# Inverse deviations by a GpSimd power, resident FFN weights from the third set of tokens on, and new constants in the planner's time model

## The chip, the cores and the metric

The kernel runs on one core of a Trainium2 chip. The metric is the device time of one execution in microseconds (us), as the median of several runs. The engines are named as in the profile: PE (TensorE, matmuls), PEld (its weight loads), DVE (VectorE), ACT (ScalarE), POOL (GpSimd) and SP (SyncE, which here issues nearly all DMAs). Each engine executes its own instructions in order and waits on semaphores for the others.

## The reference

One transformer block with modulation from a condition vector, for 2048 tokens of width 512, with 32 heads of 16 and an FFN of width 1792, in bfloat16:

```python
x = A_x
mod = (_silu(c) @ w_mod).reshape(c.shape[0], 6, 1, -1)
sa, ca, ga, sb, cb, gb = (mod[:, i] for i in range(6))
h = _layernorm(x, axis=-1) * (1 + ca) + sa
x = x + ga * _A_ref(h, A_wqkv, A_wo)        # softmax attention over all 2048 keys, then wo
h = _layernorm(x, axis=-1) * (1 + cb) + sb
x = x + gb * _B_ref(h, B_w_gate, B_w_up, B_w_down)
# _B_ref: _gelu(x @ w_gate) * (x @ w_up) @ w_down, with the tanh form of gelu
# _layernorm: (x - m) / sqrt(v + 1e-5), over the 512 of a token
```

## The kernel before

The program is written by a recorder. `rec` (L190) takes every instruction with what it reads and writes, works out the semaphores that it needs, and gives it a start and an end in a time model (`model`, L278). The order of the instructions of each engine is the order in which they are recorded, and a greedy planner (`stream`, L1224) chooses it: at each step it probes what each candidate would have to wait for in the model, and records one. A DMA's landing in the model is the end of the modelled DMA plus `LAND`, and the modelled DMA moves 350 bytes a nanosecond. Nothing of the plan is decided at run time.

The tokens are cut into sets of 512, 512, 512, 256, 128 and 128 queries (`SETS`). A unit is one set (the last two together for most heads) with four of the eight groups of heads; its scores come in rounds of four items, an item being 512 scores on all 128 partitions, in PSUM. There are 2048 items. Normally PE makes three of them, ACT takes their exps in one instruction (128 x 1536, PSUM to the SBUF tile `E`), and PE multiplies them with the values (`ps_pv`). Some rounds, called quads, go to DVE instead: it makes an approximate exp of each of the four items through a uint16 conversion (into the tiles `kq`, in `mreg` and `dreg`), and three shifted copies of 128 x 2048 uint16 (`shift_task`), which DVE or POOL makes and which PE multiplies with the values too. `QA` and `QB` say which tiles of keys may be treated so: a round must lie within them. `AHEAD` says how many items ahead of the current one a quad's round must lie at least. A quad is opened only where DVE is free in the model and one of three `kq` buffers is; after the scores of the third set (`ends[2]`), also only if the side work's credit is below `CREDIT` or its next matmul is not ready within `IDLE` (2000 ns, the flag `idle`).

Everything else is side work in the gaps of the attention: first the projections, then, for each set that is done, the output projection (`side_wo`), the second layernorm (`ln2_steps`) and the FFN (`side_ffn`), in the order and with the due times of `plan` (L1137). Small steps for DVE, ACT and SP are tasks, which `step` records when the model says that they would not wait. Softmax denominators go through DRAM: SP stores the sums (`scr_den<-osb`), loads them back spread over partitions (`den<-scr_den`), DVE takes reciprocals (`rden`), SP stores them (`scr_rec<-rden`) and loads them broadcast (`rb<-scr_rec`); then DVE makes the normalised output (`onorm`).

The inverse deviation of a layernorm (`ln_rstd`, L641, and `ln_rstd_step`, L627) is eight DVE instructions: a first guess through the bits of the number, then two Newton steps of three. It is called for four tiles of 128 tokens, or for as many as a set has, ten times in all.

An FFN of a set below `FLOW` (4) streams its weights: seven blocks of 256 KB of each of gate, up and down; gate and up through two buffers each (`wst`, in `mreg`), down into `wdst`. The last two sets use weights that stay (`wg`, `wu`, `wd`), 21 blocks, which `more_weights` loads once the third and the fourth FFN are done; the FFN of the fifth set waits for all of them (the key `weights`):

```python
    def more_weights(self):
        for parts, k in ((self.early, 2), (self.late, 3)):
            if parts and ("ffn", k) in self.have:
                parts.pop(0)()
                if not self.late:
                    self.done("weights")
                return True
        return False
```

They lie in memory that the attention no longer needs: the gate blocks in `qT` (queries of the first three sets), the down blocks in `xs` (tokens that have been put out), the up blocks in the streaming buffers.

After the last P·V comes `tail` (L1594): the fifth set's FFN, whose output projection, layernorm and transposes (`t2T`) must be recorded before it (the key `part`), and the sixth set's output projection, layernorm and FFN.

Of the kernel before, what the change touches and what calls it, by code (L numbers as in the profile page):

```python
# [13 lines left out]
P = 128  # L14
# [28 lines left out]
AHEAD = 24  # L43
PREFER = 300
LAND = 1500
# [10 lines left out]
QA = 6  # L56
QB = 13
FLOW = 4
# [37 lines left out]
class _Recorder:  # L96
# [181 lines left out]
    def model(self, op, t, cost):  # L278
        eng = op.eng
        if op.stream not in COMPUTE:  # L280
            self.free[eng] = t + 460
            self.dma_free = max(t + 1400, self.dma_free) + cost / 350
            op.t1 = self.dma_free + LAND
# [176 lines left out]
class _Kernel(_Recorder):  # L460
# [12 lines left out]
    def alloc(self):  # L473
# [25 lines left out]
        self.wdst = [dreg[:, a * D:(a + 2) * D] for a in (8, 10, 12)] + [mreg[:, a * D:(a + 2) * D] for a in (2, 0, 6, 4)]  # L499
        self.wdst = [a.rearrange("p (f n) -> p f n", f=2) for a in self.wdst]  # L500
        self.wg = [self.qT[:, :, 256 * i:256 * i + 256] for i in range(6)]
        self.wg.append(hreg[:, NFC * 256:NFC * 256 + 1024].rearrange("p (a n) -> p a n", a=NDC))
        self.wu = [self.wst[i // 2][i % 2] for i in range(4)]
        self.wu += [dreg[:, 1024 * i:1024 * i + 1024].rearrange("p (a n) -> p a n", a=NDC) for i in range(4, 7)]
        self.wd = [self.xs[:, 2 * i:2 * i + 2, :] for i in range(6)]
        self.wd.append(hreg[:, NFC * 256 + 1024:NFC * 256 + 2048].rearrange("p (f n) -> p f n", f=2))
# [15 lines left out]
        self.nwx = sb("nwx", [P, NT], FP32)  # L522
# [20 lines left out]
    def prologue(self):  # L543
# [19 lines left out]
        self.memset(dve, self.ones, 1.0)  # L563
        self.memset(dve, self.pv[:, :], 0.0)
# [60 lines left out]
    RSTD = 8  # L625

    def ln_rstd_step(self, a, b, i):  # L627

        x, y, t = self.nwx[:, a:b], self.rstd[:, a:b], self.nwt[:, a:b]
        if i == 0:  # L630
            self.ts("dve", x, self.mv[:, a:b, 1], EPS, -0.5, ALU.add, ALU.mult)
        elif i == 1:
            self.ts("dve", y.bitcast(I32), x.bitcast(I32), -0.5, 1597463007.0 - 2.0 ** 30 - 2.0 ** 22, ALU.mult, ALU.add)
        elif i % 3 == 2:
            self.tt("dve", t, y, y, ALU.mult)
        elif i % 3 == 0:
            self.tt("dve", t, t, x, ALU.mult)
        else:
            self.stt(y, t, 1.5, y, ALU.add, ALU.mult)

    def ln_rstd(self, a, b):  # L641
        for i in range(self.RSTD):
            self.ln_rstd_step(a, b, i)
# [145 lines left out]
    def side_first(self):  # L789
# [4 lines left out]
        def norms(t0):  # L794
            g = t0 // 4
            self.task([lambda i=i: self.ln_rstd_step(t0, t0 + 4, i) for i in range(self.RSTD)]
                      + [lambda t=t: self.ln_norm(t0 + t, self.tb1[:, g % 2, t, :]) for t in range(4)], ("ln", g),
                      self.after([("st", t) for t in range(max(8, t0), t0 + 4)]))
# [65 lines left out]
    def weight_parts(self):  # L864

        def part(dst, src, sem):
            return lambda: self.dma("sp", dst, src, sem)
# [3 lines left out]
        a = [part(self.wg[i], gv[:, :, 256 * i:256 * i + 256], "wg%d" % i) for i in range(7)]  # L871
        a += [part(self.wd[i], dv[:, 2 * i:2 * i + 2, :], "wd%d" % i) for i in range(7)]
        b = [part(self.wu[i], uv[:, :, 256 * i:256 * i + 256], "wu%d" % i) for i in range(7)]
        return a, b
# [4 lines left out]
    def ln2_steps(self, k, src=None):  # L879

        a, b = SETS[k][0] // P, sum(SETS[k]) // P
        return ([lambda i=i: self.ln_rstd_step(a, b, i) for i in range(self.RSTD)]
# [48 lines left out]
    def side_wo(self, gi):  # L931
# [14 lines left out]
        if not self.dry:  # L946
            self.done(("wo", gi))
            steps = self.ln2_steps(gi)
            self.task(steps[:self.RSTD], ("rs", gi), self.after([("st2", t) for t in tiles]))
            self.task(steps[self.RSTD:], ("ln2", gi), self.after([("rs", gi)] + [("ffn", gi - 1)] * (gi > 0)))  # L950

    def side_ffn(self, gi, part=None):
# [7 lines left out]
        flow = gi < FLOW  # L960
        kpb = 512 // W
# [5 lines left out]
        def load(x, ci):  # L967
            if flow and ci < len(chunks) and not self.dry:
# [9 lines left out]
        if flow:  # L978
            for i in range(2):
                load(0, i)  # L980
                load(1, i)
        yield from self.until(("ln2", gi))
        if not flow:
            yield from self.until("weights")
# [4 lines left out]
        def up(x, ci, sub):  # L989
            for s, fc in enumerate(sub):  # L990
                for dci in range(NDC):
                    if flow:
# [6 lines left out]
        def G(ci):  # L999
# [3 lines left out]
            if flow:  # L1003
                yield from self.until(("ld", gi, 0, ci))
# [13 lines left out]
        def U(ci):  # L1018
# [4 lines left out]
            if flow:  # L1023
                yield from self.until(("ld", gi, 1, ci))
            for b0 in range(0, m, kpb):
# [22 lines left out]
        if part is not None:  # L1048
            self.done(("part", gi))
            return  # L1050
        for i in range(n):
            for fc in range(NFC):
                yield 512, lambda i=i, fc=fc: self.mm(
                    mi, prod[:, fc, P * i:P * i + P], self.wdst[fc // 2][:, fc % 2, :], start=(fc == 0), stop=(fc == NFC - 1))
# [62 lines left out]
    def background(self, t):  # L1117
        if POOLED and self.free["pool"] < t and self.busy():
            self.pooled(t)
        while self.step("sp", max(self.free["sp"], t) + 40):  # L1120
            pass
        while self.free["dve"] <= t + 150 and self.step("dve", max(self.free["dve"], t) + 40):
            pass

    def force(self):
        assert any(self.step(e, None) for e in ("dve", "sp", "act")) or self.more_weights()

    def more_weights(self):
        for parts, k in ((self.early, 2), (self.late, 3)):
            if parts and ("ffn", k) in self.have:  # L1130
                parts.pop(0)()
                if not self.late:
                    self.done("weights")
                return True
# [611 lines left out]
```

## Time and profile before

| | us |
|---|---|
| median of 8 runs | 820.86 (818.78 to 823.49) |
| the profiled execution | 819.25 |
| its span in the profile | 817.5 |
| ACT's last exp of scores ends | 790.9 |
| outputs of set 3 (256 tokens) go out | 768.3 and 774.9 |
| outputs of set 2 go out | 696.7 to 720.7 |

The page in forty slices of 20.4 us; each digit is a busy share in tenths, and the last row is what the DMA moved:

```profile
DVE  7978999988898989998898999998887998776574
ACT  4999999999999999999999999999999999998972
POOL 1000623353362323614443424233020000000000
...
GB/s 313 50 8 12 16 10 16 10 16 10 15 61 34 55 59 36 59 42 23 28 61 54 35 60 34 61 41 22 30 22 117 61 62 64 23 210 208 89 95 15
```

A group's row later in the text reads: line, engine, operation, tile written and tiles read, shape, count, then busy time in us and the mean of one in ns, then the engine's idle time before these instructions and what ended it. Since a helper records each operation, all instructions of one kind have one line, and the tiles tell them apart. In a view of one tile, three numbers after a count are the shortest, the median and the longest in ns. A row of a stretch has its start and end, its length, and for each engine the busy time and the count, then PE's granted clock, the share of time in which the DMA engines were busy, and GB/s.

### The profile page before, as it was taken

Reading aid. Unit: us, or ns where it says so; the run is one execution under the profiler, and the core shown is the slowest. Engines: PE = TensorE matmul, PEld = TensorE weight load, DVE = VectorE, ACT = ScalarE, POOL = GpSimd, SP = SyncE. Lnnn points to the kernel's source line nnn. Section 1 sums busy time; section 2 is a strip of 40 time slices with the busy share of each in tenths; the row PEclk is TensorE's granted clock in tenths of the full one; section 3 lists DMA queues with packets and bytes.
Section 4 is the critical chain, followed back from the end, with each engine's and each line's share of the span. In section 5 each row is a group of like instructions: output and inputs, shape, how many; then the busy total and the mean of one; then the engine's idle time right before and its main releaser. Section 6 shows DMA issues by size and latency. Waiting matters only on the chain.

```text
span 817.5 us, 27542 instructions
## 1 busy us (share of the span) xinstructions
PE 752.6 (92%) x12273; PEld 268.6 (33%) x12278; DVE 695.6 (85%) x1320; ACT 779.7 (95%) x734; POOL 204.9 (25%) x118
## 2 busy tenths in 40 slices
PE   8899999999898899999998899999998899998988
PEld 3333333322222222222222222222343343445456
DVE  7978999988898989998898999998887998776574
ACT  4999999999999999999999999999999999998972
POOL 1000623353362323614443424233020000000000
PEclk9999999999999999999999999999999999999999
DMA  9100000000021121210122121210104222077330
GB/s 313 50 8 12 16 10 16 10 16 10 15 61 34 55 59 36 59 42 23 28 61 54 35 60 34 61 41 22 30 22 117 61 62 64 23 210 208 89 95 15
DMA packets 74569, 45.74 MB, mean 56 GB/s; under 512 B 18553, under 2 KB 71026, under 8 KB 74450
## 3 DMA queue, kind: packets, MB, share of 16 engines
q1 hardware_dynamic: 72066, 42.41, 18.8%
q8 instruction: 96, 1.57, 0.8%
q10 hardware_dynamic: 2384, 1.57, 0.7%
q14 instruction: 23, 0.19, 0.1%
HBM read 39.31 MB, written 2.61 MB: 51 GB/s over the span
## 4 chain that ended last, share of the span: by engine, by line
ACT 73%; PE 14%; DMA 5%; DVE 5%; SPq 3%; issue 1%; DVEq 0%
ACT E L367 70%; PE ps_mi L354 6%; PE ps_sc L354 6%; SPq L418 3%; ACT wreg L367 2%; PE ps_pv L354 2%; DMA mreg<-in_B_w_up_dram 1%; DMA scr_rec<-rden 1%; DMA mreg<-in_w_mod_dram 1%; DMA mreg<-in_B_w_gate_dram 1%; DVE mreg L379 1%; DMA den<-scr_den 1%; DVE wreg L371 1%; DMA scr_den<-osb 0%; DVE wreg L379 0%
## 5 line engine op out<-in xcount | busy, mean ns | idle before, releaser
L367 ACT ACTIVATE E<-ps_sc 128x1024 bf16<-128x1024 f32 (+2 forms) x687 | 751.2, 1271 | 22.4 <-PE ps_sc L354 21.6
L379 POOL TENSOR_SCALAR mreg<-dreg 128x2048 uint16<-128x2048 uint16 x78 | 146.8, 1897 | 257.5 <-PE ps_pv L354 53.9
L379 DVE TENSOR_SCALAR dreg<-ps_sc 128x512 uint16<-128x512 f32 x247 | 168.0, 687 | 28.0 <-PE ps_sc L354 25.1
L354 PE MATMUL ps_sc<-qT,kme 32*128 32x512 bf16 (+2 forms) x1321 | 166.3, 331 | 15.6 <-ACT E L367 13.7
L354 PE MATMUL ps_sc<-qT,kmo 32*128 32x512 bf16 (+2 forms) x1315 | 166.9, 332 | 12.1 <-ACT E L367 11.1
L354 PE MATMUL ps_pv<-E,vaug 128*17 128x512 bf16 (+2 forms) x2132 | 152.1, 327 | 1.3 <-DVE vaug L388 0.8
L354 PE MATMUL ps_mi<-wreg,mreg 128*32 128x512 bf16 (+1 forms) x1792 | 118.0, 359 | 11.6 <-DVE wreg L384 4.1
L354 PE MATMUL ps_pv<-mreg,vaug 128*17 128x512 bf16 (+2 forms) x1644 | 119.8, 342 | 3.1 <-DVE mreg L379 1.9
L379 DVE TENSOR_SCALAR mreg<-ps_sc 128x512 uint16<-128x512 f32 x129 | 87.9, 687 | 17.4 <-PE ps_sc L354 16.1
L354 PEld LDWEIGHTS ps_sc<-qT,kme 32*128 32x128 bf16 x1321 | 44.1, 91 | 138.7 <-ACT E L367 115.8
L354 PEld LDWEIGHTS ps_sc<-qT,kmo 32*128 32x128 bf16 x1315 | 44.1, 91 | 133.9 <-ACT E L367 111.0
L379 DVE TENSOR_SCALAR mreg<-dreg 128x2048 uint16<-128x2048 uint16 x129 | 84.6, 684 | 1.4 <-PE ps_pv L354 1.1
L379 POOL TENSOR_SCALAR mreg<-mreg 128x2048 uint16<-128x2048 uint16 x29 | 54.6, 1898 | 87.7 <-DVE mreg L379 66.2
L354 PEld LDWEIGHTS ps_pv<-E,vaug 128*17 128x17 bf16 x2132 | 45.0, 89 | 62.4 <-issue 50.6
L354 PEld LDWEIGHTS ps_mi<-wreg,mreg 128*32 128x32 bf16 x1792 | 40.0, 96 | 59.0 <-issue 17.0
L379 DVE TENSOR_SCALAR mreg<-mreg 128x2048 uint16<-128x2048 uint16 x76 | 51.0, 694 | 0.8 <-PE ps_pv L354 0.7
L354 PEld LDWEIGHTS ps_pv<-mreg,vaug 128*17 128x17 bf16 x1644 | 36.7, 89 | 37.2 <-DVE mreg L379 11.9
L384 DVE SCALAR_TENSOR_TENSOR wreg<-wreg,ps_mi 128x512 bf16<-128x512 bf16 x49 | 33.5, 683 | 8.2 <-PE ps_mi L354 5.8
L354 PE MATMUL ps_mi<-hreg,wreg 128*32 128x512 bf16 x480 | 39.7, 385 | 0.5 <-DVE qT L379 0.2
L388 DVE CAST wreg<-ps_mi 128x512 bf16<-128x512 f32 x49 | 33.6, 686 | 7.3 <-PE ps_mi L354 6.8
L354 PE MATMUL ps_mi<-mreg,hreg 128*32 128x512 bf16 x448 | 36.8, 384 | 0.0
L371 DVE TENSOR_TENSOR wreg<-wreg 128x1024 bf16<-128x1024 bf16 (+1 forms) x56 | 34.4, 620 | 0.5
(151 smaller groups left out, 607.3 us busy)
## 6 DMA issues: line engine op xcount, KB each, us to landing
mreg<-in_B_w_up_dram SPq DMA_DIRECT2D x32, 256.0 KB, 3.4
mreg<-in_B_w_gate_dram SPq DMA_DIRECT2D x28, 256.0 KB, 3.2
mreg<-in_B_w_down_dram SPq DMA_DIRECT2D x16, 256.0 KB, 2.7
rb<-scr_rec SPq DMA_DIRECT2D x96, 32.0 KB, 1.8
dreg<-in_B_w_down_dram SPq DMA_DIRECT2D x12, 256.0 KB, 4.0
mreg<-in_w_mod_dram SPq DMA_DIRECT2D x1, 2048.0 KB, 14.5
out_dram<-xs SPq DMA_DIRECT2D x16, 128.0 KB, 1.7
osb<-osb SPq DMA_DIRECT2D x48, 32.0 KB, 2.0
```

What stands on the lines that cost most here:

```text
L354: return self.rec("pe", lambda e: e.matmul(out, lhsT, rhs, start=start, stop=stop, tile_position=tp), [lhsT, rhs], [out], cost=(n, int(rhs ...
L367: return self.rec("act", lambda e: e.activation(out, in_, func, scale=scale, **kw), rd, wr, cost=self.cost("act", out, [in_], "act"))
L371: return self.rec(eng, lambda e: e.tensor_tensor(out, a, b, op), [a, b], [out], cost=self.cost(eng, out, [a, b], "tt"))
L379: return self.rec(eng, lambda e: e.tensor_scalar(out, a, s1, s2, **kw), rd, [out], cost=self.cost(eng, out, [a], "ts"))
L384: return self.rec("dve", lambda e: e.scalar_tensor_tensor(out, a, s, b, op0=op0, op1=op1), rd, [out], cost=self.cost("dve", out, [a, b], " ...
L388: return self.rec(eng, lambda e: e.tensor_copy(out, in_), [in_], [out], cost=self.cost(eng, out, [in_], "ts"))
L418: return e.dma_start(out, in_)
```

## The change

`ln_rstd` becomes two POOL instructions, an addition of epsilon and a power of -0.5 against a constant tile `half`; they are recorded as tasks of POOL, which `background`, `force` and `tail` now serve. The two are not entered in the list that keeps DVE and POOL apart (`port`).

`FLOW` becomes 2. The first two FFNs stream as before. The third streams only its up blocks and takes gate and down from the resident ones; the fourth takes all from them. A new function, `resident`, makes the loads tasks of SP, each due at a position of the attention (in items after `ends[2]`, `SPACE` = 12 apart, gate first, then down, then up) and, where the memory is in use until then, after an FFN. Two of the seven up blocks are those that the third FFN streamed last. The resident blocks move: down into `xs` and `dreg`, up into `xs`, `hreg` and the streaming buffers.

In the time model a DMA that starts after 20 us moves 175 instead of 350 bytes a nanosecond and lands 800 instead of 1500 ns after that. `QA` becomes 5 (so `vaug2`, the scaled values, has eight tiles of keys instead of seven), and `AHEAD` 20.

```diff
-AHEAD = 24
+AHEAD = 20
-LAND = 1500
+LAND = 800
+RATE = 175
+POW = (350, 145)
+SPACE = 12
-QA = 6
+QA = 5
-FLOW = 4
+FLOW = 2
...
-            self.dma_free = max(t + 1400, self.dma_free) + cost / 350
-            op.t1 = self.dma_free + LAND
+            early = t < 20000
+            self.dma_free = max(t + 1400, self.dma_free) + cost / (350 if early else RATE)
+            op.t1 = self.dma_free + (1500 if early else LAND)
...
+        stay = [two(dreg[:, a * D:(a + 2) * D]) for a in (8, 10, 12)]
+        self.wdst = stay + [two(mreg[:, a * D:(a + 2) * D]) for a in (2, 0, 6, 4)]
+        self.wg = [self.qT[:, :, 256 * i:256 * i + 256] for i in range(6)] + [self.wst[0][0]]
+        self.wd = [self.xs[:, 2 * i:2 * i + 2, :] for i in range(4)] + stay
+        self.wu = [self.wst[0][1]] + [four(self.xs[:, 8 + 2 * i:10 + 2 * i, :].rearrange("p t n -> p (t n)")) for i in range(2)]
+        self.wu += [four(hreg[:, NFC * 256 + 1024 * i:NFC * 256 + 1024 * i + 1024]) for i in range(2)]
+        self.wu += [self.wst[1][1], self.wst[1][0]]
...
     def ln_rstd(self, a, b):
-        for i in range(self.RSTD):
-            self.ln_rstd_step(a, b, i)
+        out, v = self.rstd[:, a:b], self.mv[:, a:b, 1]
+        self.rec("pool", lambda e: e.tensor_scalar(v, v, EPS, None, op0=ALU.add), [v], [v], cost=200)
+        c = self.half[:, 0:b - a]
+        self.rec("pool", lambda e: e.tensor_tensor(out, v, c, ALU.pow), [v, c], [out], cost=POW[0] + POW[1] * (b - a))
...
+    def resident(self, pos):
...
+        def part(name, i, dst, src, p, key=None):
+            self.task([("sp", lambda: self.dma("sp", dst, src, "w%s%d" % (name, i)))], ("ld", name, i),
+                      lambda: self.pos >= p and (key is None or key in self.have))
+        for i in range(6):
+            part("g", i, self.wg[i], gv[:, :, 256 * i:256 * i + 256], pos + SPACE * i)
+        part("g", 6, self.wg[6], gv[:, :, 1536:1792], pos + SPACE * 6, ("ffn", FLOW - 1))
+        for i in range(7):
+            part("d", i, self.wd[i], dv[:, 2 * i:2 * i + 2, :], pos + SPACE * (8 + 2 * i), ("ffn", FLOW - 1))
+        for i in range(5):
+            part("u", i, self.wu[i], uv[:, :, 256 * i:256 * i + 256], pos + SPACE * 22, ("ffn", FLOW - (i == 0)))
...
+        half = gi == FLOW
...
-            if flow and ci < len(chunks) and not self.dry:
+            if (flow or (half and x == 1)) and ci < len(chunks) and not self.dry:
...
-        if not flow:
-            yield from self.until("weights")
+        if part is not None:
+            for i in range(5):
+                yield from self.until(("ld", "u", i))
...
-            if flow:
-                yield from self.until(("ld", gi, 0, ci))
+            yield from self.until(("ld", gi, 0, ci) if flow else ("ld", "g", ci))
...
-            if flow:
+            if flow or half:
                 yield from self.until(("ld", gi, 1, ci))
+            elif ci < 5:
+                yield from self.until(("ld", "u", ci))
...
+        wd = self.wdst if flow else self.wd
+        for i in range(0 if flow else 7):
+            yield from self.until(("ld", "d", i))
...
+        self.step("pool", max(self.free["pool"], t) + 40)
...
-        self.early, self.late = self.weight_parts()
+        self.resident(ends[2])
         while cg <= group[units[-1]]:
-            if pos >= loaded and self.more_weights():
-                loaded = pos + 3
```

## The prediction, made before the changed kernel was run

> **What bounds the kernel now.** I read the page's totals first, then the busy time by stretch of the span, then what ScalarE waited for, and last the DMA queue beside the end of the attention.
>
> From the page, busy time by engine and the chain of waits:
>
> ```profile
> PE 752.6 (92%) x12273; PEld 268.6 (33%) x12278; DVE 695.6 (85%) x1320; ACT 779.7 (95%) x734; POOL 204.9 (25%) x118
> ...
> ACT 73%; PE 14%; DMA 5%; DVE 5%; SPq 3%; issue 1%; DVEq 0%
> ```
>
> ScalarE (ACT) is the bound: its exps of the scores are 70% of the chain. The same work by stretch (busy us of PE, PEld, DVE, ACT, POOL; granted clock; DMA share; GB/s):
>
> ```profile
> 40.00:580.00 540.00, 504.63 (x7224) 152.38 (x7227) 483.64 (x848) 539.11 (x512) 195.90 (x105) 1.00 0.13 34
> 580.00:720.00 140.00, 129.89 (x2570) 51.44 (x2566) 113.92 (x219) 138.00 (x120) 5.62 (x3) 1.00 0.21 55
> 720.00:791.00 71.00, 62.14 (x1685) 34.15 (x1682) 51.20 (x112) 66.42 (x59) 0.00 (x0) 0.98 0.61 170
> 791.00:817.50 26.50, 21.77 (x281) 16.94 (x286) 14.34 (x35) 7.06 (x13) 0.00 (x0) 1.00 0.04 11
> ```
>
> Between 40 and 580 us ACT idles 0.9 us of 540: only moving exps to VectorE (DVE) shortens that stretch. From 720 to 791 ACT idles 4.6 us while the DMA is busy 61% of the time, against 13% and 21% before. In 610 to 640 us it idles another 1.9. The last 26.5 us are the tail: FFNs of the last two tiles, PE busy 21.77 of them. So three things can shorten the run: fewer exps on ACT, fewer stalls after 580, an earlier start of the tail.
>
> What ACT and PE waited for in 720 to 791 us (total, times, longest):
>
> ```profile
> ACT E L367 <- PE ps_sc L354: 4.4, 6, 1.6
> PE ps_mi L354 <- DMA mreg<-in_B_w_up_dram: 1.8, 2, 1.2
> PE ps_mi L354 <- DMA mreg<-in_B_w_gate_dram: 1.8, 1, 1.8
> ```
>
> ACT waits for scores; PE, which executes in order, was standing at FFN matmuls whose weights had not landed. In the twenty-microsecond rows, 740 to 760 also has a granted clock of 0.91.
>
> **The weights.** Before, four FFNs stream 21 blocks of 256 KB each and the tail loads 21 more: 105 loads (32+28+16+12+6+6+3+1+1 in the page's DMA table). After, FFNs 0 and 1 stream 42, FFN 2 its 7 up blocks, and 19 resident blocks are loaded once (7 gate, 7 down, 5 up; the other two up blocks are FFN 2's last, left in place): 68. So 37 loads, 9.7 MB, go. What matters is where. In FFN 2's stretch 21 become 22, with the gate and down blocks spread by 12 and 24 items. After FFN 2 (at 720.7 us) 42 become 4.
>
> Does spreading add a wait? The fourth set's eight units end between 603.6 and 681.3 us (their denominator stores), 256 items in 77.7 us, 0.30 us an item. The last down block is issued 240 items after the end of set 2's scores; if that is 8 us before its last store, at about 595, it is 668 us. Before, FFN 2's first output went out at 696.7 and the outputs are some 8 us apart, so its down product began near 689. The new wait for all seven down blocks therefore has some 15 us of cover with a 3 us landing; without it FFN 2 alone would stand (attention goes on), and FFN 3 behind it. FFN 3 needs up blocks 1 to 4 after 720.7: 1 MB, at the 260 GB/s of 720 to 740 us 4 us, beside its first gate chunks.
>
> So the DMA stalls of 720 to 791 should go. Of ACT's 4.4 us I take 3.0, as DMA waits of PE add up to 3.6 and some of PE's time will be wanted elsewhere. In 610 to 640, four streamed loads are issued ahead of a denominator store (610.7 to 612.98); two of the four stay, so I take 1.0 of 1.9. **Term a: 4.0 us** (ends 0, PE becomes the wait, and 6.3, all of both).
>
> **The tail's start.** SyncE's queue at the end of the attention, and how long a reciprocal's store took to land there and in 612 to 720 us:
>
> ```profile
> 775.29 1.59 SPq L418 DMA_DIRECT2D mreg<-in_B_w_up_dram  x3
> 776.92 0.50 SPq L418 DMA_DIRECT2D scr_rec<-rden  x1
> 777.47 0.44 SPq L418 DMA_DIRECT2D mreg<-in_B_w_up_dram  x1
> 777.95 1.15 SPq L418 DMA_DIRECT2D dreg<-in_B_w_up_dram  x2
> 781.41 1.72 SPq L418 DMA_DIRECT2D rb<-scr_rec  x4
> ...
> scr_rec<-rden SPq DMA_DIRECT2D x1, 4.0 KB, 4.5
> ...
> scr_rec<-rden SPq DMA_DIRECT2D x9, 4.0 KB, 1.4
> ```
>
> The reciprocals were ready at 775.2, but three up-weight loads stood ahead on SyncE until 776.9, and the store then took 4.5 us instead of 1.4. That is 1.7 + 3.1 = 4.8 us on the path to set 4's output projection, layernorm and transposes, whose last modulate ends at 793.2, with the tail's first FFN matmul just behind. All seven loads leave this place. The gain is capped: ACT's last exps end at 790.9 whatever the weights do, and the last P·V follows them. So at most 793.1 − 791.0 = 2.1 us; I take **term b: 1.0 us** (ends 0 and 2.1).
>
> **The inverse deviations.** Ten calls of eight small DVE instructions:
>
> ```profile
> L384 DVE SCALAR_TENSOR_TENSOR rstd<-nwt,rstd 128x4 f32<-128x4 f32 (+2 forms) x20 | 3.1, 160 | 0.4
> L371 DVE TENSOR_TENSOR nwt<-rstd 128x4 f32<-128x4 f32 (+2 forms) x20 | 3.1, 159 | 0.4
> L371 DVE TENSOR_TENSOR nwt<-nwt,nwx 128x4 f32<-128x4 f32 (+2 forms) x20 | 3.1, 159 | 0.4
> L379 DVE TENSOR_SCALAR rstd<-nwx 128x4 int32<-128x4 int32 (+2 forms) x10 | 1.6, 163 | 0.2
> L379 DVE TENSOR_SCALAR nwx<-mv 128x4 f32<-128x4 f32 (+2 forms) x10 | 1.6, 155 | 0.1
> ...
> L398 POOL TENSOR_SCALAR_AFFINE_SELECT den<-den 128x4 f32<-128x4 f32 x2 | 0.4, 189 | 0.1
> ```
>
> That is 12.5 us of DVE, 1.25 a call; with the gaps between dependent steps a call lasts 1.54 us (7.24 to 8.78). Of the ten, one is in the prologue, three in 16 to 40 us, four in 40 to 720, one at 789 and one in the tail. Seven stand in stretches where DVE could take exps instead: 7 × 1.54 = 10.8 us. A "quad" of rounds on DVE costs 4 exps of 0.69 us and three shifted copies, of which DVE makes 205 of 312: 4 × 0.69 + 1.97 × 0.69 = 4.1 us. It takes four items from ACT at 1.27/3 = 0.42 us (ten exps of three items last 12.69 us at 774.2), 1.7 us. All of it turned into quads would be 10.8/4.1 × 1.7 = 4.5 us. The low end is 0: the freed slots are 1.5 us pieces, and DVE already idles 56 of the 540 us.
>
> No row shows a power on GpSimd (POOL). From below, two instructions like the 0.19 us select, 0.4 us; from above, two like POOL's 2048-element shift, 3.8 us. I take 1.1 us, nearer the small row, for four elements are not 2048. Behind it on POOL stand only shifts that other rounds hide. In the prologue the norms end at 10.2 and the modulation columns are ready at 10.9, so an equal POOL chain changes nothing: 0 (ends: gain 0.7, loss 2.3). In the tail the call takes 2.1 us (797.69 to 799.79, one other DVE instruction in it) while PE runs set 4's FFN: I take 0.5.
>
> Here a rule of the Trainium skill speaks against the change. *SBUF — State Buffer*, "Which ops grab the shared pair" and the points around it: GpSimd and a DVE instruction in a two-port mode, or with two SBUF inputs, lock each other out for a whole instruction. The kernel keeps its shifts apart with a port list, but the power is recorded without the lock, so nothing plans around it. The trace shows what a collision costs:
>
> ```profile
> L379 DVE TENSOR_SCALAR mreg<-mreg x76: 628/686/1490, 42.8 to 776.3; 128x2048 uint16<-128x2048 uint16 x76
> ```
>
> One shift took 1490 ns instead of 686. By the rule, if each of seven powers caught such an instruction, DVE would lose 7.7 of the 10.8 us and the gain would fall to 3.1/4.1 × 1.7 = 1.3 us. By the rows, such instructions (shifts 135.6 us, products of two SBUF tensors about 70) fill a quarter of DVE's span, so about 2 us are lost and 3.6 of 4.5 us remain possible. I take **term c: 2.3 us**, half of the 4.5, for both reasons, and 0.5 for the tail's call.
>
> **The constants.** A slower modelled DMA with an earlier landing moves the recorded order, since the planner places work when it thinks data is there; QA 5 gives each unit of 16 rounds eight instead of seven that DVE may take, and AHEAD 20 lets them be taken later. DVE's use is 90% in 40 to 580 us, so more candidates alone need not mean more quads. I put these at 0, with ±4 us.
>
> **Sum.** 4.0 + 1.0 + 2.3 + 0.5 = 7.8 us. The profiled execution, span 817.5 in a run of 819.25, becomes 809.7 in 811.4; the median before was 1.6 above that run, so the forecast is **813.0**.
>
> **The rivals.**
> - *The loads were hidden anyway* (0.18): ACT's idle time after 720 moves from DMA waits to PE, which has FFN 3 to do and is busy 20.0 of 20 us in 700 to 720. Only 2.3 and 0.5 remain: 818.1. For it: the wait is always a PE row. Against: PE is busy only 17.0 and 18.0 us in 720 to 760.
> - *More goes to DVE* (0.17): all freed time becomes quads (4.5) and the wider choice gives one more quad per set's eight units (3 × 1.7), with the other terms: 4.0 + 1.0 + 0.5 + 4.5 + 5.1 = 15.1, so 805.8.
> - *Slower: late quads vanish* (0.12). After set 2 a quad is opened only if the FFN's credit is low or its next matmul is not ready within 2 us (`idle`). In 580 to 791 us DVE made 66 exps (36 + 22 + 8), 16.5 quads. With weights always resident, `idle` is true less often; if 8 quads are lost, ACT gets 13.6 us and the sum is 5.8 worse: 826.7. It decides from 4.6 quads lost. Against it: a faster FFN also lowers its credit, which opens quads.
> - *The power is slow* (0.03): several us a call in POOL's order, no gain from c and a longer tail: about 818.
>
> **How the numbers follow.** The forecast's own case has 0.50, with 808 to 818. From no change this kernel's measurement tells 0.3%, 2.5 us: 818.4 and 823.3. The range 804 to 820 takes in the more-on-DVE and hidden cases and leaves out most of the slow one. Faster: 0.50 + 0.17 + half of the hidden case, 0.09, and some of the rest, 0.83; same 0.08; slower 0.09.
>
> **What would show it.** Loads 68 and some 36 MB; no PE wait for a weight DMA after 720; ACT idle of 720 to 791 near 1.5 us; the five groups of small DVE instructions gone and ten POOL pairs near 1 us in their place; DVE exps above 416 (424 for two more quads); the reciprocal's store before the tail landing in about 1.5 us; the tail 1 to 2 us shorter. Wrong would be: fewer exps than 416, PE standing before FFN 2's down product, or shifts stretched beyond 0.69 us beside the powers.

## The result, and the profile after

| | before | after |
|---|---|---|
| median, us | 820.63 (33 runs) | 813.29 (12 runs, 811.3 to 818.85) |
| span of the profiled execution, us | 817.5 | 810.2 |
| first exp of scores starts | 16.72 | 15.98 |
| ACT idle between the first and the last of these exps | 8.73 | 6.87 |
| end of the exps (start of the table load behind them) | 790.93 | 783.77 |
| from there to the end (the tail) | 26.59 | 26.39 |
| exps on DVE, of 2048 items | 416 | 424 |
| median granted PE clock (110 runs of before in the later comparisons, 13 of after) | 0.995 | 0.998 |

The ratio is 0.9915 [0.99, 0.9931]: 7.3 us faster, where 7.8 were forecast. From the page of after: busy time by engine, two of the rows in forty slices (here of 20.3 us), and the chain of waits.

```profile
PE 752.5 (93%) x12297; PEld 266.9 (33%) x12302; DVE 685.7 (85%) x1246; ACT 775.1 (96%) x729; POOL 233.4 (29%) x147
...
ACT  5999999999999999999999999999989999999982
...
GB/s 309 57 9 13 15 10 15 10 17 10 16 62 65 30 54 48 35 41 30 29 30 101 22 54 47 60 30 29 74 47 81 47 67 57 22 75 14 16 15 14
...
ACT 65%; PE 17%; DVE 10%; DMA 4%; SPq 2%; issue 1%; POOL 0%; DVEq 0%; POOLq 0%
```

The block of 210, 208 and 89 GB/s near the end is gone. ACT is still the bound, with 4.6 us less work (779.7 before). The 8 on its row, in the thirtieth slice, is new; before, the low slices lay near the end. The same by stretch:

```profile
40.00:580.00 540.00, 508.49 (x7223) 151.41 (x7215) 478.45 (x828) 538.68 (x510) 221.06 (x121) 1.00 0.13 35
580.00:720.00 140.00, 128.61 (x2568) 51.77 (x2560) 111.60 (x205) 135.64 (x116) 2.21 (x4) 1.00 0.21 56
720.00:783.80 63.80, 59.12 (x1672) 32.39 (x1660) 52.48 (x108) 63.75 (x59) 0.81 (x2) 1.00 0.10 23
783.80:810.20 26.40, 21.78 (x281) 16.83 (x284) 12.94 (x26) 7.10 (x13) 0.80 (x2) 1.00 0.03 11
```

Behind 720 us ACT idles 0.05 of 63.8 us, where it was 4.6 of 71, and the DMA's share fell from 0.61 to 0.10. From 580 to 720 it idles 4.4 us, where it was 2.0. What ACT waited for there (total, times, longest):

```profile
ACT E L371 <- PE ps_sc L358: 4.2, 2, 4.0
```

Nearly all of it is one stall. The chain of waits through it (start, length, what), and then PE and DVE at its end in order of time, with the idle time before an instruction in brackets:

```profile
586.71 0.36 SPq L422
587.07 0.04 issue
587.11 2.28 DMA scr_rec<-rden
...
590.69 2.86 DMA rb<-scr_rec
593.55 0.03 issue
...
593.67 0.70 DVE onorm L375
```

```profile
592.50 0.82 PE L358 MATMUL ps_mi<-wo,onorm 128*32 128x512 bf16 x12
593.67 0.69 DVE L375 TENSOR_TENSOR onorm<-osb,rb 128x512 bf16<-128x512 f32 x1 [3.40 <-DMA rb<-scr_rec]
594.42 0.40 PE L358 MATMUL ps_mi<-wo,onorm 128*32 128x512 bf16 x4 [1.10 <-DVE onorm L375]
...
595.71 2.91 ACT L371 ACTIVATE E<-ps_sc 128x1024 bf16<-128x1024 f32 x3 [3.97 <-PE ps_sc L358]
```

PE makes twelve output-projection matmuls and then stands 1.10 us for the last normalised output, with P·V and the next scores queued behind. Most of the rest of ACT's 3.97 us PE spends on side work that was recorded ahead of those scores, these twelve matmuls among it. DVE had stood 3.40 us for the broadcast reciprocals. Their last load landed 2.86 us after its issue; the planner's new model gives it 1400 + 187 (32 KB at 175 bytes a nanosecond) + 800 ns, 2.39 us. That these 0.47 us are the cause is not shown: `after_l780` below, whose model lands 20 ns earlier still, has no such stall.

The inverse deviations on POOL and the shifts on DVE beside them (the first two are groups; in the last, the numbers after the count are shortest, median and longest ns):

```profile
L633 POOL TENSOR_SCALAR mv<-mv 128x4 f32<-128x4 f32 (+2 forms) x10 | 2.3, 230 | 243.9 <-DVE mv L415 236.7
...
L635 POOL TENSOR_TENSOR rstd<-mv,half 128x4 f32<-128x4 f32 (+2 forms) x10 | 9.3, 934 | 0.8
```

```profile
L635 POOL TENSOR_TENSOR rstd<-mv,half x10: 577/1037/1222, 7.9 to 789.9; 128x4 f32<-128x4 f32 x7, 128x1 f32<-128x1 f32 x2, 128x2 f32<-128x2 f32 x1
```

```profile
L383 DVE TENSOR_SCALAR mreg<-mreg x75: 643/687/789, 43.0 to 773.2; 128x2048 uint16<-128x2048 uint16 x75
```

A pair for four tiles costs 0.23 + 1.04 us. No shift is longer than 789 ns, and that one, at 568.6 us, has a shift on POOL beside it and no power. Only one power of after has a shift on DVE beside it:

```profile
239.77 1.22 POOL L635 TENSOR_TENSOR rstd<-mv,half 128x4 f32<-128x4 f32 x1
...
240.27 0.68 DVE L383 TENSOR_SCALAR mreg<-dreg 128x2048 uint16<-128x2048 uint16 x1
```

There the power took 1222 ns instead of 1037, and the shift its usual 684. Two more powers, at 29.3 and 618.7 us, have products of two SBUF tensors on DVE beside them; neither is stretched (1037 and 1036 ns), nor are those products (354, 352 and 416 ns, as elsewhere).

Last, the start of the tail, before and then after: DVE's addition behind the fifth set's output projection, and the table load that follows ACT's last exp.

```profile
787.54 0.69 DVE L371 TENSOR_TENSOR xs<-xs,ps_mi 128x512 bf16<-128x512 bf16 x1 [1.18 <-PE ps_mi L354]
...
790.93 1.28 ACT L367 ACT_TABLE_LOAD   x1
```

```profile
779.87 0.69 DVE L375 TENSOR_TENSOR xs<-xs,ps_mi 128x512 bf16<-128x512 bf16 x1 [1.27 <-PE ps_mi L358]
...
783.77 1.28 ACT L371 ACT_TABLE_LOAD   x1
```

Both came forward together, by 7.7 and 7.2 us. The end of the addition less the end of the exps, called the **lag** from here, went from -2.7 to -3.2 us, and the tail stayed as it was.

### The profile page after: what moved, and what is told of

Its sections match the earlier page's. It is cut to its first block, busy times and chain, and to the rows that moved or that the text cites. A ratio compares the mean times of both kernels' runs of the same rounds, so it can differ in the third digit from the quotient of the medians.

```text
span 810.2 us, 27514 instructions
## 1 busy us (share of the span) xinstructions
PE 752.5 (93%) x12297; PEld 266.9 (33%) x12302; DVE 685.7 (85%) x1246; ACT 775.1 (96%) x729; POOL 233.4 (29%) x147
## 2 busy tenths in 40 slices
DMA packets 58616, 36.03 MB, mean 44 GB/s; under 512 B 17961, under 2 KB 55074, under 8 KB 58498
## 3 DMA queue, kind: packets, MB, share of 16 engines
q1 hardware_dynamic: 56114, 32.71, 14.5%
## 4 chain that ended last, share of the span: by engine, by line
ACT 65%; PE 17%; DVE 10%; DMA 4%; SPq 2%; issue 1%; POOL 0%; DVEq 0%; POOLq 0%
ACT E L371 63%; PE ps_mi L358 7%; PE ps_sc L358 6%; PE ps_pv L358 3%; DVE mreg L383 2%; ACT wreg L371 2%; SPq L422 2%; DVE dreg L383 1%; DVE wreg L388 1%; DMA rb<-scr_rec 1%; DVE wreg L392 1%; DMA mreg<-in_w_mod_dram 1%; DVE wreg L375 1%; DMA den<-scr_den 1%; DMA scr_rec<-rden 1%
## 5 line engine op out<-in xcount | busy, mean ns | idle before, releaser
L371 ACT ACTIVATE E<-ps_sc 128x1024 bf16<-128x1024 f32 (+1 forms) x682 | 747.2, 1284 | 19.4 <-PE ps_sc L358 18.8
L383 POOL TENSOR_SCALAR mreg<-dreg 128x2048 uint16<-128x2048 uint16 x83 | 156.1, 1898 | 204.8 <-DVE mreg L383 89.6
L383 DVE TENSOR_SCALAR dreg<-ps_sc 128x512 uint16<-128x512 f32 x244 | 165.8, 686 | 32.6 <-PE ps_sc L358 31.2
L358 PE MATMUL ps_sc<-qT,kme 32*128 32x512 bf16 (+2 forms) x1316 | 170.3, 331 | 12.9 <-ACT E L371 10.6
L358 PE MATMUL ps_pv<-E,vaug 128*17 128x512 bf16 (+2 forms) x2120 | 148.8, 326 | 1.0 <-DVE vaug L392 0.8
L358 PE MATMUL ps_pv<-mreg,vaug 128*17 128x512 bf16 (+2 forms) x1688 | 124.0, 341 | 1.8 <-DVE mreg L383 1.3
L358 PE MATMUL ps_mi<-wreg,mreg 128*32 128x512 bf16 (+1 forms) x1280 | 90.6, 372 | 4.8 <-DVE wreg L388 2.3
L383 DVE TENSOR_SCALAR mreg<-ps_sc 128x512 uint16<-128x512 f32 x124 | 84.0, 686 | 10.8 <-PE ps_sc L358 9.6
L383 POOL TENSOR_SCALAR mreg<-mreg 128x2048 uint16<-128x2048 uint16 x33 | 62.2, 1897 | 83.9 <-DVE mreg L383 56.7
L358 PEld LDWEIGHTS ps_mi<-wreg,mreg 128*32 128x32 bf16 x1280 | 26.7, 95 | 43.6 <-issue 17.4
L358 PE MATMUL ps_sc<-xs,ident 128*32 128x512 bf16 x332 | 25.8, 384 | 13.3 <-ACT E L371 12.5
```

The lines of the kernel that those rows point to most:

```text
L358: return self.rec("pe", lambda e: e.matmul(out, lhsT, rhs, start=start, stop=stop, tile_position=tp), [lhsT, rhs], [out], cost=(n, int(rhs ...
L371: return self.rec("act", lambda e: e.activation(out, in_, func, scale=scale, **kw), rd, wr, cost=self.cost("act", out, [in_], "act"))
L383: return self.rec(eng, lambda e: e.tensor_scalar(out, a, s1, s2, **kw), rd, [out], cost=self.cost(eng, out, [a], "ts"))
```

## The experiments

The theory at the start: resident weights take the stalls behind 720 us away, the power lets DVE take two more quads, and the constants do little. The rival: what changed is mainly the recorded order, and the parts can't be summed. Each kernel below was measured beside before once more, whose median was then 819.8 to 820.3 us; the ratios are against that, so they compare better than the medians.

**One part at a time.** The kernel before with the power alone, with the resident weights alone, with the constants alone; and the kernel after with the deviations back on DVE.

```diff
# pow_only: before, and
-            self.task([lambda i=i: self.ln_rstd_step(t0, t0 + 4, i) for i in range(self.RSTD)]
+            self.task([("pool", lambda: self.ln_rstd(t0, t0 + 4))]
...
# res_only: before, and resident() with all it touches, with the constants
-FLOW = 4
+FLOW = 2
+RATE = 350
+SPACE = 12
# const_only: before, and
-AHEAD = 24
+AHEAD = 20
-LAND = 1500
+LAND = 800
+RATE = 175
-QA = 6
+QA = 5
# no_pow: after, and
-        self.rec("pool", lambda e: e.tensor_tensor(out, v, c, ALU.pow), [v, c], [out], cost=POW[0] + POW[1] * (b - a))
+        for i in range(self.RSTD):
+            self.ln_rstd_step(a, b, i)
```

> The kernel before with the power on POOL alone. If the terms of the prediction add up, 2.3 us for exps that move to DVE and 0.5 in the tail: some 2.8 us less than before, 817.8; its recorded program has 424 exps on DVE against 416, so ACT's exps should be busy 3.4 us less. If the power's exclusive use of the port eats the freed DVE time, within 1 us of before, and DVE's two-port instructions beside a power last over 1 us. If plan luck rules, anything from -4 to +4.

> The kernel before with the resident weights alone (deviations on DVE, time model, QA and AHEAD as before). By the prediction 5.0 us less than before (4.0 from stalls after 580 us, 1.0 from the tail's start), 815.6, and no wait of PE for a weight DMA after 720 us. If the loads were hidden anyway, within 1 us of before. 420 exps on DVE are recorded, so up to 1.7 us of the gain may be those.

> The kernel before with RATE, LAND, QA and AHEAD of the change alone. The prediction put these at 0 with 4 us to both sides: 820.6, 816.6 to 824.6. If the more accurate landing times help the order, 2 us or more below before; if a modelled landing that is too early makes PE stand at matmuls recorded too soon, above before.

> The changed kernel with the deviations on DVE again. If terms add up, 2.8 us above the changed kernel, 816.1. If the power gives its gain only through two more rounds of exps on DVE, about 1.7 us (420 exps recorded against 424). If plan luck rules, it can be on either side of 813.3 by some us.

Measured: `pow_only` 821.9 us, ratio 1.0032 [1.0015, 1.0049]; `res_only` 817.0, 0.997 [0.9959, 0.9982]; `const_only` 841.97, 1.0277 [1.0241, 1.0312]; `no_pow` 823.87, 1.0055 [1.0036, 1.0073]. Against the profiled span of before that is +2.2, -2.5, +22.1 and +4.4 us; the three parts sum to +21.8, and together they gave -7.3. The sums had put the four at 817.8, 815.6, 820.6 and 816.1 us. The parts do not add.

Two readings hold in spite of that. With the power alone the waits behind 720 us stay (ACT's, then PE's, total, times, longest):

```profile
ACT E L368 <- PE ps_sc L355: 6.7, 6, 2.1
```

```profile
PE ps_mi L355 <- DMA mreg<-in_B_w_up_dram: 2.1, 1, 2.1
...
PE ps_mi L355 <- DMA mreg<-in_B_w_gate_dram: 2.0, 1, 2.0
```

and in `res_only` ACT idles 0.0 us there. So the resident weights took those stalls away, not the power. But `res_only` kept only 2.5 us, since its tail is 32.7 us. Its trace in order of time:

```profile
782.37 1.28 ACT L371 ACT_TABLE_LOAD   x1
...
784.01 0.69 DVE L375 TENSOR_TENSOR xs<-xs,ps_mi 128x512 bf16<-128x512 bf16 x1 [0.79 <-PE ps_mi L358]
...
787.70 0.28 PE L362 MATMUL ps_mi<-ident,hreg 128*128 128x128 bf16 x2 [3.74 <-DVE hreg L383]
...
792.73 0.60 ACT L371 ACTIVATE E<-ps_sc 128x512 bf16<-128x512 f32 x1 [8.87 <-PE ps_sc L358]
```

The exps ended 8.6 us earlier than before, but the fifth set's addition now comes behind them (lag +2.3), and its layernorm and transposes follow with PE idle 3.74 us. `pow_only` (lag +1.2, tail 32.6; PE waits 3.09 us there) and `no_pow` (+1.6, 32.4; 3.73 us) are alike. In `const_only` the lag is 10.8 and the tail 42.5, and ACT idles 22.3 us in all, of it 14.5 in two waits behind 720. Its last exp of scores ends at 789.3, 1.6 us earlier than before's; the second wait (7.2 us) and one step of FFN 3 stand between that and the table load at 797.1. PE waits for no DMA there behind 700 us, so it does not stand for data that the model took to have landed; FFN 3 is still under way behind the exps.

New theory: a second chain sets the tail. PE does the fifth set's output projection behind FFN 3; if that is recorded late, the tail is longer, whatever ACT does. And which lag comes out is an accident of the recorded order. If so, a change with no meaning of its own must move the time too.

**Only the order.** `LAND` moved by 20 to 100 ns, or `AHEAD` put back. The values were chosen because the planner's own model ended early with them (of `before_l1520`, to see a small step on the kernel before), so these are picked from the scatter, not drawn from it.

```diff
# before_l1520: before, and
-LAND = 1500
+LAND = 1520
# pow_l1600: pow_only, and
-LAND = 1500
+LAND = 1600
# res_l1450: res_only, and
-LAND = 1500
+LAND = 1450
# after_l780: after, and
-LAND = 800
+LAND = 780
# after_l750: after, and
-LAND = 800
+LAND = 750
# no_pow_l850: no_pow, and
-LAND = 800
+LAND = 850
# after_a24: after, and
-AHEAD = 20
+AHEAD = 24
```

> The kernel before with LAND 1520 instead of 1500: a change of 20 ns in the planner's idea of a landing, which removes and adds no work. If the orders that the planner finds scatter, and the tail's length follows how late the fifth set's output projection comes (26.5 us when it is 3 us before the last exps, 31 us plus the delay when it is after them, as in the runs so far), this plan, which records it some 9 us after, is 8 to 14 us slower than before: 829 to 835. If the single runs so far show the worth of their parts, within 2 us of before.

> The changed kernel with LAND 780 instead of 800, again no change of the work. Its plan records the fifth set's output projection well before the last exps, so by the tail's law the tail stays at 26.5 us; the exps end some 3 us earlier in the plan and the stall of 4.0 us near 592 us may go: 808 to 812. If the changed kernel's order doesn't depend on such details, 813.3 within 1 us.

> The kernel before with the power alone, in an order (LAND 1600) that records the fifth set's output projection before the last exps, as before and after do. If pow_only (821.9) was slow only because its tail was 32.6 us instead of 26.5, this one keeps the earlier end of its exps (3.9 us) with a short tail: 814 to 818. If the power on POOL itself costs, it stays at 820 or more.

> The kernel before with the resident weights alone, in an order (LAND 1450) with the fifth set's output projection before the last exps. If the long tail (32.7 us) hid the gain of res_only, whose exps ended 8.6 us earlier, this one comes to 809 to 814. If the resident weights are worth only the 2.8 us seen, 816 to 818.

> The changed kernel with the deviations on DVE, in an order (LAND 850) that records the fifth set's output projection some 6 us before the last exps. By the tail's law it loses the 6 us of no_pow's long tail: 812 to 818 instead of 823.9, so that the power is worth 2 to 6 us, not the 10.6 between no_pow and the changed kernel. If the power is worth 10 us, it stays at 820 or more.

> The changed kernel with LAND 750, chosen among some forty such orders as one that the planner itself thinks short. By the tail's law 808 to 812, with a tail under 26.5 us; if orders matter less than it seems, 813.3.

> The changed kernel with AHEAD at its old 24, all else as changed. If AHEAD 20 is part of the gain, above 813.3; if it only picks another order, and this one has the output projection of the fifth set some 5 us before the last exps, 808 to 812. 424 exps on DVE are recorded in both.

All fourteen kernels (lag, tail and ACT's idle time from the profiled execution; "pow", "res" and "const" say which parts a kernel has). The end of the exps is again the start of the table load; only in `const_only` does that differ from the last exp of scores, from which its lag is 18.7, its tail 50.4 and its idle time 15.1.

| kernel | parts | median us | ratio [interval] | lag | tail | ACT idle | DVE exps |
|---|---|---|---|---|---|---|---|
| before | | 820.63 | 1 | -2.7 | 26.6 | 8.7 | 416 |
| before_l1520 | | 835.71 | 1.0194 [1.0164, 1.0224] | 9.6 | 40.1 | 13.5 | 420 |
| pow_only | pow | 821.9 | 1.0032 [1.0015, 1.0049] | 1.2 | 32.6 | 9.6 | 424 |
| pow_l1600 | pow | 817.37 | 0.9961 [0.9948, 0.9974] | -2.0 | 26.7 | 10.5 | 424 |
| res_only | res | 817.0 | 0.997 [0.9959, 0.9982] | 2.3 | 32.7 | 3.1 | 420 |
| res_l1450 | res | 812.31 | 0.9905 [0.9881, 0.993] | -2.2 | 27.5 | 2.5 | 420 |
| const_only | const | 841.97 | 1.0277 [1.0241, 1.0312] | 10.8 | 42.5 | 22.3 | 432 |
| no_pow | res, const | 823.87 | 1.0055 [1.0036, 1.0073] | 1.6 | 32.4 | 9.6 | 420 |
| no_pow_l850 | res, const | 812.15 | 0.9913 [0.9886, 0.994] | -5.2 | 25.7 | 3.6 | 420 |
| after | all | 813.29 | 0.9915 [0.99, 0.9931] | -3.2 | 26.4 | 6.9 | 424 |
| after_l780 | all | 809.67 | 0.9887 [0.9854, 0.9921] | -6.5 | 25.4 | 5.1 | 424 |
| after_l750 | all | 810.44 | 0.9901 [0.9872, 0.9931] | -2.0 | 26.7 | 5.6 | 428 |
| after_a24 | all but `AHEAD` | 811.56 | 0.991 [0.988, 0.9939] | -4.5 | 25.7 | 5.5 | 424 |
| double_pow | all, power twice | 820.73 | 1.0012 [0.9996, 1.0029] | -3.2 | 27.4 | 13.1 | 424 |

Six of the seven came out in the range expected for the short or long tail; `before_l1520` was 0.7 us above its own. `AHEAD` back at 24 costs nothing: `after_a24` is not slower than after. Twenty nanoseconds of a modelled landing cost the kernel before 15 us. Its tail in order of time:

```profile
793.95 1.28 ACT L367 ACT_TABLE_LOAD   x1
...
798.85 1.90 PE L354 MATMUL ps_mi<-mreg,hreg 128*32 128x512 bf16 x32
...
802.86 0.69 DVE L371 TENSOR_TENSOR xs<-xs,ps_mi 128x512 bf16<-128x512 bf16 x1 [0.91 <-PE ps_mi L354]
...
806.54 0.39 PE L358 MATMUL ps_mi<-ident,hreg 128*128 128x128 bf16 x2 [3.74 <-DVE hreg L379]
```

FFN 3's down product runs on PE until 800.7 us, after ACT's last exp, and only behind it come the fifth set's output projection and the same chain with the same 3.74 us. Over the table, the tail is 25.4 to 27.5 us where the lag is -2.0 or less, and about 30 to 32 us plus the lag where the addition comes behind the exps. So the second chain sets the tail there.

A part of the longer tails is PE's clock. In all five kernels with a lag above zero the granted clock falls to 0.50 in the tail, in PE's wait for that layernorm or just behind it, for 6.8 us (3.4 in `res_only`); in the nine others it is 1.00 from the end of the exps to the last output. `pow_only`, as a row of a stretch:

```profile
790.54:797.37 6.83, 5.70 (x37) 4.62 (x39) 3.54 (x9) 0.60 (x1) 0.00 (x0) 0.50 0.44 126
```

As an estimate, half of PE's busy time in such a stretch, here 2.9 us, would be saved at full clock. The two orders with the power and a lag of -2.0 have a tail of 26.7, that is, 28.7 us plus the lag. With this estimate added (1.4 to 2.9 us), that sum gives each of the five long tails within 0.3 us; `res_l1450`, with a short one, lies 1.0 us above it, so it is good to about 1 us.

Compared among orders with a short tail, the parts look different: the power alone is worth 3.2 us (0.39%), the resident weights alone 7.8 us (0.95%), the weights with the new constants 7.1 us (0.87%), and everything between 7.0 and 9.3 us. In `res_l1450` ACT's idle time fell by 6.2 us, and behind 720 us little is left of it:

```profile
ACT E L371 <- PE ps_sc L358: 0.2, 1, 0.2
```

So in these orders the resident weights are the main gain. What the power adds on top of them lies inside the scatter of the orders. `after_l780` has none of the 4 us stall at 592 us (ACT idles 0.1 us from 580 to 640). At 0.9887 it is faster than before beyond doubt and has the lowest median of all; against after itself the two intervals overlap, so that step is likely and not certain.

**The power's exposure.** Every power of after is made twice, first into a tile that nobody reads, with no cost in the model; the recorded orders of PE, DVE, ACT and SP stay the same.

```diff
+        x = self.more[:, a:b]
+        self.rec("pool", lambda e: e.tensor_tensor(x, v, c, ALU.pow), [v, c], [x], cost=0)
```

> The changed kernel with each power made twice, the first into a tile that nobody reads, at no cost in the planner's model, so that every other engine's order is that of the changed kernel: it prices the power. One takes 1.04 us for four tiles and 0.58 for one or two, ten together 9.3 us. If they lie beside other work, only the first and the one of the fifth set count, 0.3 to 0.6 us each: 813.5 to 815. If each stands on the path or locks DVE out, 9 us more: 822.

Measured: 820.73 us, 7.4 more than after, for 9.3 us more of POOL's time; that is above the 813.5 to 815 expected for hidden powers and near the 822 for exposed ones. By the ratios the difference is 8.0 us. DVE's costliest group of waits for the power (total, times, longest), in after and then in `double_pow`:

```profile
DVE dreg L383 <- POOL rstd L635: 1.5, 1, 1.5
```

```profile
DVE dreg L383 <- POOL rstd L638: 4.9, 4, 2.5
```

The slip of ACT's instructions against after's is 2.5 us after the four calls ahead of 40 us, 3.3 at 433, 2.9 at 491, and then goes to 8.1 us between 622 and 629. That last step is not what it looks like. In order of time:

```profile
621.62 1.04 POOL L637 TENSOR_TENSOR more<-mv,half 128x4 f32<-128x4 f32 x1
...
622.62 1.01 POOL L638 TENSOR_TENSOR rstd<-mv,half 128x4 f32<-128x4 f32 x1
...
623.96 0.20 DVE L395 RECIPROCAL rden<-den 128x8 f32<-128x8 f32 x1 [1.67 <-DMA den<-scr_den]
...
624.63 1.37 DVE L383 TENSOR_SCALAR hreg<-xs,mv,rstd 128x512 bf16<-128x512 bf16 x4
...
627.37 1.45 ACT L371 ACTIVATE E<-ps_sc 128x1536 bf16<-128x1536 f32 x1 [1.83 <-PE ps_sc L358]
```

DVE stood for a load of denominators that took 3.6 us to land (1.6 us at the same place of after), and the second power had ended before it, at 623.63. The pauses of PE around it were followed by half the granted clock for 10.2 us, and the stretch from 620 to 640 us shows a clock of 0.74:

```profile
620.00:640.00 20.00, 17.83 (x272) 7.32 (x268) 13.25 (x28) 15.53 (x13) 2.25 (x3) 0.74 0.16 41
```

That made all runs be sorted by their mean granted clock. Within one kernel, span and clock go together (correlation -0.83 over 110 runs of before, -0.90 over 13 of after, -0.91 over 22 of `double_pow`), at 0.61 to 0.69 us for each thousandth of clock. Read off the fitted lines at a clock of 1.000, the span is 815.2 us for before, 809.8 for after and 814.3 for `double_pow`. So some 4.5 of its 7.4 us remain at equal clock, 0.45 us a call, and the rest goes with the clock (median 0.9925 against 0.998). A lower clock can itself follow from pauses that a change makes, so the part at equal clock need not be all that the powers cost: the runs can't tell whether the later powers make PE's pauses likelier or the median fell that way by chance in one set of 22.

## Why the prediction was right, point by point

The total was right by errors that cancel. Between the two profiled executions ACT idled 1.9 us less, had 4.6 us less work up to the table load, started its exps 0.7 us earlier and left a tail 0.2 us shorter: 7.4, where the terms were 4.0 for stalls, 2.3 for exps, nothing for the start and 1.5 for the tail.

- **The weights, term a (4.0 us): right mechanism, wrong size.** 68 loads and 36.03 MB, as counted. No wait for a weight is left behind 720 us, and all 4.6 us of ACT's stalls there went, where I took 3.0 of 4.4: the doubt that PE "will be wanted elsewhere" was not borne out. The cover of FFN 2's down blocks held: they were issued from 610 to 667 us, and its first output went out at 693.5. From 610 to 640 all 1.9 us went too, where I took 1.0. What the term left out is a new stall: with the new order 4.0 us stand at 592, and ACT's idle time from 580 to 640 rose from 1.9 to 4.0. Net 1.9 us instead of 4.0. Without that stall, in `res_l1450`, 6.2 us were to be had, nearly the upper end of 6.3 that the term named.
- **The tail, terms b (1.0) and the tail's call (0.5): both came to nothing, 0.2 together.** The reciprocal's store landed in 2.1 us instead of 4.5, and the chain came 7.7 us earlier; but the exps came 7.2 us earlier too. The sum counted the chain as if the exps would stay at 790.9 (and its cap, from the 793.2 and 790.9 given beside it, is 2.3 us, not 2.1). That a lag above about -2 us costs tail the parts alone show (+1.2 to +10.8); whether the earlier store is what kept the lag of after at -3.2 is not shown.
- **The power, term c (2.3).** The pair took 1.27 us where 1.1 was put. The reading of the rows (about 2 us lost) was nearer than the 7.7 us that the rule of the Trainium skill's *SBUF — State Buffer* gives for seven collisions. Three of the ten powers met an instruction of the rule's kinds; one was stretched, by 0.19 us, and DVE's instructions not at all. In `pow_only` two powers beside a shift took 1416 and 1546 ns and the shifts 683 and 693, so what these meetings stretched was the power. Exps on DVE went to 424, two quads or 8 × 0.42 = 3.4 us of ACT; the whole fall of ACT's work is 4.6, and the rest of it was not traced. With the power alone there are 424 too, but kernels with the new weights and without the power already have 420, so on top of the weights the power bought one quad, 1.7 us. That the term's 2.3, half of the 4.5, lies near this is luck, and ACT's work fell by twice that: the sum held no quad for the order.
- **The prologue (0).** The first exp came 0.74 us earlier. The power isn't the reason: the same 32 matmuls of the projection took less, because PE's clock in before's execution was halved for 3.4 us from 11.8 on. Before, then after:

```profile
12.02 3.46 PE L354 MATMUL ps_sc<-hreg,wreg 128*32 128x512 bf16 x32
```

```profile
12.36 2.39 PE L358 MATMUL ps_sc<-hreg,wreg 128*32 128x512 bf16 x32
```

- **The constants (0, ±4 us): the term that failed.** Its bounds were too narrow by far. Alone they cost 2.8% (22.7 us), and 20 ns of `LAND` cost 15. The zero was luck: the order of the full change was one with a short tail. Among orders with a short tail the weights without the constants and with them differ by 0.7 us (7.8 and 7.1).
- **The clock, which the sum left out.** I read 0.98 behind 720 us and 0.91 from 740 to 760 and gave them no term. In before the clock was half from 749.1 to 752.5, and 1.9 of ACT's 4.4 us came in it and just behind it (at 751.5 and 753.6), while PE was busy 5.0 of the 5 us from 750 on: there it no longer stood for weights but worked off what it had missed, at first at half the clock. The two are not told apart. By the fitted lines 5.4 of the 7.3 us are at equal clock and 1.9 come with the higher clock of after (median 0.998 against 0.995).
- **The rivals.** "Hidden anyway" falls: ACT idles 0.0 us behind 720 in `res_only` and 0.2 in `res_l1450`. "More goes to DVE" falls: 8 more exps, where that case needs some 23 (4.5 + 5.1 us at 0.42). "Late quads vanish" falls: 16.75 quads from 580 us on, where before had 16.5. "The power is slow" falls as to its length; but it is exposed in part: DVE waits for it three times, 3.1 us in all; made twice, DVE waits seven times, 8.3 us, and some 4.5 us are lost at equal clock. The way to "slower" that the parts did take, the fifth set's chain behind FFN 3, was not among my rivals; the profile before showed it (addition at 788.2, exps at 790.9), and the cap of 2.1 us in term b set this chain's later steps (793.1) against the end of the exps without asking what a chain 3 us later would do.

Open: how much of each kernel's time belongs to its parts and how much to its order (each point of the table is one order, and picked); `QA` and `RATE` were never moved alone.

## What to carry to other kernels

Where a greedy planner fixes the order, an edit is measured together with an accident: record several orders of each version by a step that means nothing, look at what ends last in each, and compare like with like before a part is given a price. When two chains meet at the end of a stage (here ACT's exps and the fifth set's output projection), write both times down: a gain on one is worth what the other leaves, and a small slip of the hidden one can turn the sign. And a stall of PE is priced with the clock that follows it, so sort a kernel's runs by granted clock before a difference of a per cent is explained, and look in the traces whether the change itself made the pauses.

## What the runs showed of the hardware that was not expected

- A power on POOL takes 577 ns for 128x1, some 0.7 us for 128x2 and 1037 ns for 128x4, so about 0.15 us an element of a partition: the 128x4 power takes 4.5 times the addition's mean of 230 ns.
- Beside shifts or products on DVE, it was the power on POOL that lasted longer (1222 ns in after, up to 1546 in `pow_only`), if anything did.
- In `double_pow` PE's clock fell to half near 625.2 us and stayed there for 10.2 us, with PE busy nearly all of them. In the 5 us before, PE's longest pause was 0.92 us, and its pauses in the last 3.4 us add up to 1.7. The Trainium skill's *TensorE: Matmul & The Clock Gate*, Part 1, asks in its table for an idle window of about 3.4 us and lets a busy one restore the clock, and further down tells of short pauses that make the clock swing, without a figure; here half a window of pauses came before, and three windows passed. Over all fourteen traces the clock fell fifteen times between 40 us and the end of the exps, each time with 0.9 to 2.1 us of pauses in the 3.4 us before; but 2.3 us of pauses near 635 us of `const_only` passed without a fall. In two-microsecond rows of `double_pow`:

```profile
624.00:626.00 2.00, 1.25 (x13) 0.42 (x9) 2.00 (x7) 1.54 (x2) 0.00 (x0) 0.81 0.04 2
626.00:628.00 2.00, 1.97 (x28) 0.99 (x27) 1.60 (x4) 0.64 (x1) 0.00 (x0) 0.50 0.15 28
...
634.00:636.00 2.00, 2.00 (x38) 0.85 (x34) 1.40 (x3) 0.91 (x1) 0.00 (x0) 0.62 0.29 94
636.00:638.00 2.00, 2.00 (x52) 0.83 (x44) 0.79 (x2) 1.70 (x2) 0.00 (x0) 1.00 0.04 2
```

- The spread between runs of one kernel goes with PE's granted clock (correlations of -0.83 to -0.91 above): `double_pow` ran from 815.8 us at a clock of 0.998 to 826.3 at 0.983.
- Loads of 4 KB of denominators landed after 1.5 to 5.5 us in before (the slowest at 731 us, among the weight loads) and at most 3.4 us in after.
